# Eight 64x32 array tiles for the per-head products, and a token softmax by 32x32 vector transposes

## The chip, the cores and the metric

The kernel runs on one core of one Trainium2 chip. The metric is the device time of one execution in microseconds (us), as the median of several. Engines are named as the profile names them: PE (TensorE, matrix products), PEld (its weight loads), DVE (VectorE), ACT (ScalarE), POOL (GpSimd). PSUM is the memory to which PE writes the products here; its tiles take one bank or two.

## The reference

Two blocks follow one another. `x` is (8, 8, 512, 64): batch, head, token, feature; `state` is (8, 8, 32, 64).

```python
scores  = x @ state^T / 8        # (B,H,512,32): softmax over the 32 states
xread   = softmax(scores)  @ state
scores2 = state @ x^T / 8        # (B,H,32,512): the same numbers, softmax over the 512 tokens
sread   = softmax(scores2) @ x
out     = concat([xread, sread], token axis)      # 544 rows a batch
h = out.reshape(B*544, 512) @ w_in                # w_in 512 x 2048, w_out 2048 x 512, both float64
return (h * cos(h)) @ w_out
```

For token rows `xread @ w_in` is computed as `softmax(scores) @ (state @ w_in)`: the product of the states with w_in is called `sw`, and the attention weights `aT`.

## The kernel before

A main loop walks the batches in 16 steps of 128 hidden columns. In each step PE makes `h` (two matmuls) and `o` (four); DVE and ACT turn h into g = h cos h. The attention of the next batch is cut into parts that are laid into these steps.

```python
for t in tiles(b):                       # 16 steps f = 0..15
    if line: gate3(line[-1])             # g(t-1) = h * cos        DVE; frees a bank of h (two banks)
    hidden(t)                            # h(t)                    PE
    gate(t)                              # q = round(h/2pi)        DVE twice
    want = (len(work) * (t.f + 1) + NF - 1) // NF
    mid = (n_done + want + 1) // 2
    while n_done < mid:  work[n_done](); n_done += 1      # the mid place
    # ... first batch: two weight tiles are converted from float64; sw of this batch at f = 3, 7, 11
    gate2(t)                             # r, r                    DVE; then Abs, Sin  ACT
    if len(line) > 2: output(line.pop(0))                 # o(t-2) PE
    while n_done < want: work[n_done](); n_done += 1      # the late place, behind r, r
```

The attention parts the change touches (27 of them a batch, with the products):

```python
aps = tile_pool(bufs=2, PSUM)                      # a fresh bank for every part
def scores2(hb):                                   # 4 heads x 32 states on partitions
    for e in range(2):                             # 128x64 array tiles, states block by block with zeros
        matmul(out=s2[64*e:64*e+64, :], lhsT=stT[:, hb, 64*e:64*e+64], rhs=xT[:, 2*hb+e],
               tile_position=(0, 64*e))
    ...                                            # max, subtract
def scores1(ch):                                   # the same scores again, tokens on partitions
    for ci in range(2):
        for k in range(NK):
            matmul(out=s1[:, ...], lhsT=xT[:, k, 2*ch+ci, :], rhs=stT[:, k//2, ...])
    ...                                            # max, subtract
def exps(): activation(z, z, Exp, scale=scale)     # both softmaxes, one 2048-wide instruction
# sums, norm2, turn2 (transposes to a2T), norm1, turn1 (transposes to aT), reads (sT)
def products(nt, hb):                              # sw, 128x64 tiles, one bank each
    ...
```

Of the kernel before, what the change touches and what calls it, by code (L numbers as in the profile page):

```python
# [9 lines left out]
F32 = mybir.dt.float32  # L10
# [16 lines left out]
def kernel(  # L27
# [17 lines left out]
    NHB = H // 4  # L45
# [10 lines left out]
    carry = ctx.enter_context(tc.tile_pool(name="carry", bufs=2))  # L56
    gp = ctx.enter_context(tc.tile_pool(name="gp", bufs=4))
    msb = ctx.enter_context(tc.tile_pool(name="msb", bufs=3))
    osb = ctx.enter_context(tc.tile_pool(name="osb", bufs=2))
    aps = ctx.enter_context(tc.tile_pool(name="aps", bufs=2, space=PSUM))  # L60
# [12 lines left out]

    stB = consts.tile([P, B, NHB, 2 * D], F32)
    nc.vector.memset(stB, 0.0)
    ident = consts.tile([P, P], F32)
    make_identity(nc, ident)
    st_src = state.rearrange("b (hb q) n d -> q n b hb d", q=4)
    for q in range(4):
        j = q % 2  # L80
        nc.sync.dma_start(out=stB[Ns * q:Ns * q + Ns, :, :, D * j:D * j + D],
                          in_=st_src[q])
# [83 lines left out]
    def attention(b):  # L166


        x_b = x_t.pop(b)
        stT = small.tile([P, NHB, P], F32, name="stT")  # L170
        xT = asb.tile([P, NK, NC, P], F32, name="xT")


        N1 = NC * H * Ns
        z = asb.tile([P, N1 + NHB * S], F32, name="z")
        z1 = z[:, 0:N1].rearrange("p (m n) -> p m n", n=Ns)
        z2 = z[:, N1:].rearrange("p (hb t) -> p hb t", hb=NHB)
        mx = small.tile([P, NC * H + NHB], F32, name="mx")
        iz = small.tile([P, NC * H + NHB], F32, name="iz")
        a2T = asb.tile([P, NHB, NC, P], F32, name="a2T")  # L180
        aT = carry.tile([P, NHB, NC, P], F32, name="aT")
        sw = carry.tile([P, NHB, Dff], F32, name="sw")
        aT_of[b], sw_of[b] = aT, sw
        CH = NC // 2

        def states():
            st_ps = aps.tile([P, NHB, P], F32, name="at")
            for hb in range(NHB):
                nc.tensor.transpose(out=st_ps[:, hb, :], in_=stB[:, b, hb, :],
                                    identity=ident)  # L190
            nc.vector.tensor_copy(stT, st_ps)

        def tokens(k):
            xp = aps.tile([P, NC, P], F32, name="at")
            for c in range(NC):
                nc.tensor.transpose(out=xp[:, c, :],  # L196
                                    in_=x_b[:, c, 2 * k:2 * k + 2, :],
                                    identity=ident)
            nc.scalar.copy(xT[:, k], xp)  # L199

        def scores2(hb):
            s2 = aps.tile([P, S], F32, name="at")
            for e in range(2):
                nc.tensor.matmul(  # L204
                    out=s2[64 * e:64 * e + 64, :],
                    lhsT=stT[:, hb, 64 * e:64 * e + 64],
                    rhs=xT[:, 2 * hb + e].rearrange("p c t -> p (c t)"),
                    start=True, stop=True, tile_position=(0, 64 * e))
            m = mx[:, NC * H + hb:NC * H + hb + 1]
            nc.vector.reduce_max(out=m, in_=s2, axis=AX.X)  # L210
            nc.vector.tensor_scalar(z2[:, hb, :], s2, m, None, op0=ALU.subtract)  # L211

        def scores1(ch):
            s1 = aps.tile([P, CH * H, Ns], F32, name="at")
            for ci in range(CH):
                for k in range(NK):
                    e = k % 2
                    nc.tensor.matmul(  # L218
                        out=s1[:, ci * H + 2 * k:ci * H + 2 * k + 2, :],
                        lhsT=xT[:, k, CH * ch + ci, :],  # L220
                        rhs=stT[:, k // 2, 64 * e:64 * e + 64],
                        start=True, stop=True)
            ms = slice(ch * CH * H, (ch + 1) * CH * H)
            nc.vector.reduce_max(out=mx[:, ms], in_=s1, axis=AX.X)
            nc.vector.tensor_tensor(
                z1[:, ms, :], s1,
                mx[:, ms].unsqueeze(2).to_broadcast([P, CH * H, Ns]),
                op=ALU.subtract)

        def exps():  # L230
            nc.scalar.activation(z, z, func=ACTF.Exp, scale=scale)

        def sums():
            nc.vector.reduce_sum(out=iz[:, NC * H:], in_=z2, axis=AX.X)
            nc.vector.reduce_sum(out=iz[:, 0:NC * H], in_=z1, axis=AX.X)
            nc.vector.tensor_scalar(iz, iz, 1e-9, None, op0=ALU.add)
            nc.vector.reciprocal(iz, iz)

        def norm2():
            for hb in range(NHB):  # L240
                nc.vector.tensor_scalar(z2[:, hb, :], z2[:, hb, :],
                                        iz[:, NC * H + hb:NC * H + hb + 1],
                                        None, op0=ALU.mult)

        def norm1():
            nc.vector.tensor_tensor(
                z1, z1,
                iz[:, 0:NC * H].unsqueeze(2).to_broadcast([P, NC * H, Ns]),
                op=ALU.mult)


        def turn2(hb):
            tp = aps.tile([P, NC, P], F32, name="at")
            for c in range(NC):
                nc.tensor.transpose(out=tp[:, c, :],
                                    in_=z2[:, hb, P * c:P * c + P],
                                    identity=ident)
            nc.vector.tensor_copy(a2T[:, hb], tp)  # L258

        def turn1(hb):  # L260
            tp = aps.tile([P, NC, P], F32, name="at")
            for c in range(NC):
                m0 = H * c + 4 * hb
                nc.tensor.transpose(out=tp[:, c, :], in_=z1[:, m0:m0 + 4, :],
                                    identity=ident)
            nc.vector.tensor_copy(aT[:, hb], tp)



        sr = {}  # L270

        def reads(half):
            if half == 0:
                sr[0] = aps.tile([P, NK, 2 * Ns], F32, name="at")
            for k in range(2 * half, 2 * half + 2):
                e = k % 2
                for c in range(NC):
                    nc.tensor.matmul(  # L278
                        out=sr[0][:, k, :], lhsT=x_b[:, c, 2 * k:2 * k + 2, :],
                        rhs=a2T[:, k // 2, c, 64 * e:64 * e + 64],  # L280
                        start=(c == 0), stop=(c == NC - 1))
            if half == 0:
                return
            for j in range(2):
                rows = slice(D * j, D * j + D)
                nc.vector.tensor_copy(sT[rows, :, b, :],
                                      sr[0][rows, :, Ns * j:Ns * j + Ns])


        def products(nt, hb):  # L290
            ps = aps.tile([P, WC], F32, name="at")
            for e in range(2):
                nc.tensor.matmul(  # L293
                    out=ps[64 * e:64 * e + 64, :],
                    lhsT=stT[:, hb, 64 * e:64 * e + 64],
                    rhs=w_in[:, 2 * hb + e, WC * nt:WC * nt + WC],
                    start=True, stop=True, tile_position=(0, 64 * e))
            nc.scalar.copy(sw[:, hb, WC * nt:WC * nt + WC], ps)  # L298

        def part(fn, *args):  # L300
            return lambda: fn(*args)

        attn = [part(states)] + [part(tokens, k) for k in range(NK)]
        attn += [part(scores2, hb) for hb in range(NHB)]
        attn += [part(scores1, ch) for ch in range(2)]
        attn += [exps, sums, norm2]
        attn += [part(turn2, hb) for hb in range(NHB)]
        attn += [norm1]
        attn += [part(turn1, hb) for hb in range(NHB)]
        attn += [part(reads, 0), part(reads, 1)]  # L310
        prod = [part(products, nt, hb) for nt in range(NT)
                for hb in range(NHB)]
        return attn, prod
# [66 lines left out]
    def tiles(b):  # L380
        for f in range(NF):
# [3 lines left out]
            if b < B:  # L385
                t.n, t.kn, t.store = S, NHB, store_x(b)
                t.lhs = lambda i, b=b, cols=cols: sw_of[b][:, i, cols]
                t.rhs = lambda i, b=b: aT_of[b][:, i].rearrange(
                    "p c t -> p (c t)")
# [18 lines left out]

    for i, part in enumerate(attn):
        part()  # L410
        if i % 4 == 3:
            convert_to(n_conv + 1)
    convert_to(NK + 1)
    for part in prod[:NHB]:
        part()
    first = prod[NHB:]

    line = []
    for b in range(B + 1):
# [7 lines left out]
        for t in tiles(b):  # L427
# [10 lines left out]
            if b == 0:  # L438

                convert_to(NK + 1 + 2 * (t.f + 1))  # L440
                if t.f % 4 == 3:
                    for part in first[:NHB]:
                        part()
# [40 lines left out]
```

## Time and profile before

Time before: 1007.9 us (1006.7 to 1008.3). The stretches below are cut at the first h of a batch, as the trace dates it; their sum is the profiled span, 1005.8.

| stretch | us | what sets it |
|---|---|---|
| start, until h of batch 0 | 50.2 | attention of batch 0, first weight tiles |
| first batch | 172.4 | conversion of the weights on DVE, ACT and POOL |
| six batches with the next one's attention | 632.1 | PE, 6 x 105.35 |
| batch 7, no attention | 83.1 | PE |
| state rows | 68.0 | PE and the end |

The profile is read from the coarse to the fine: slices and the chain say who sets the end and when; sums over a stretch say how idle that engine is there; the timeline of one batch gives start-to-start times. In a line of a timeline, the bracket at its end is the time that the engine stood idle just before, and what ended it. The lines stand in the prediction.

### The profile page before, as it was taken

To read this page: it belongs to the slowest core of one execution; us is meant where nothing else is said; L and a number is where in the kernel's file an instruction comes from. 1 tells how busy PE (TensorE), PEld (TensorE's weight loads), DVE (VectorE), ACT (ScalarE), POOL (GpSimd) and SP (SyncE) were. 2 spreads that over 40 slices of the span, in tenths; PEclk is the share of its full clock that TensorE was granted. 3 is DMA by queue.
4 is the path that set the end of the run, shared out by engine and by line. 5 is a ranking of instruction groups with operands and counts; after the bars stand their busy time and mean duration, and the time that the engine had idled before them with its cause. 6 is when DMAs were issued, how large, how long until landed. Compare 5 with 4: busy or idle time off the path is not lost.

```text
span 1005.8 us, 7676 instructions
## 1 busy us (share of the span) xinstructions
PE 932.8 (93%) x2832; PEld 434.8 (43%) x2832; DVE 611.3 (61%) x1011; ACT 360.2 (36%) x554; POOL 88.3 (9%) x70
## 2 busy tenths in 40 slices
PE   4657768699999999999999999999999999999997
PEld 2422324234443455345534454354434443444564
DVE  3567877676754576457644784458446754566553
ACT  2354645553323332343223423233223323222322
POOL 0444444530000000000000000000000000000000
PEclk9576969799999999999999999999999999999999
DMA  8242222401020101010020002010001000100100
GB/s 188 82 128 83 84 84 84 125 1 42 1 42 0 42 0 30 13 42 1 1 42 22 21 1 42 0 42 0 1 1 42 1 1 0 42 0 1 42 1 21
DMA packets 45029, 35.09 MB, mean 35 GB/s; under 512 B 36544, under 2 KB 36544, under 8 KB 44992
## 3 DMA queue, kind: packets, MB, share of 16 engines
q1 hardware_dynamic: 44992, 34.61, 12.3%
q8 instruction: 22, 0.36, 0.1%
q14 instruction: 15, 0.12, 0.0%
HBM read 25.69 MB, written 8.91 MB: 34 GB/s over the span
## 4 chain that ended last, share of the span: by engine, by line
PE 82%; DVE 10%; ACT 3%; POOL 2%; issue 1%; DMA 1%; SPq 0%; POOLq 0%; ACTq 0%
PE o L358 44%; PE h L322 23%; PE at L293 6%; PE at L278 3%; PE at L218 2%; DVE e L155 2%; DVE e L138 2%; DVE r L340 1%; POOL w_in L158 1%; PE at L204 1%; PE at L196 1%; DVE e L153 1%; DVE q L328 1%; DVE fr L144 1%; DVE r L338 1%
## 5 line engine op out<-in xcount | busy, mean ns | idle before, releaser
L358 PE MATMUL o<-w_out,g 128*128 128x512 f32 x1088 | 498.5, 600 | 0.5 <-ACT ot L364 0.5
L358 PEld LDWEIGHTS o<-w_out,g 128*128 128x128 f32 x1088 | 200.8, 191 | 250.4 <-issue 243.5
L322 PE MATMUL h<-aT,sw 128*128 128x512 f32 x512 | 251.5, 614 | 10.7 <-DVE g L348 10.7
L342 ACT ACTIVATE r<-r 128x512 f32<-128x512 f32 (+1 forms) x144 | 87.4, 607 | 383.7 <-DVE r L340 383.7
L348 DVE TENSOR_TENSOR g<-h,r 128x512 f32<-128x512 f32 (+1 forms) x144 | 94.8, 658 | 152.2 <-ACT r L343 151.8
L328 DVE TENSOR_SCALAR q<-h 128x512 f32<-128x512 f32 (+1 forms) x144 | 94.8, 658 | 112.1 <-PE h L322 111.4
L322 PEld LDWEIGHTS h<-aT,sw 128*128 128x128 f32 x512 | 93.2, 194 | 126.0 <-issue 88.7
L340 DVE SCALAR_TENSOR_TENSOR r<-q,r 128x512 f32<-128x512 f32 (+1 forms) x144 | 103.8, 721 | 4.9
L293 PE MATMUL at<-w_in,stT 128*64 128x512 f32 x256 | 82.4, 669 | 22.7 <-DVE a2T L258 6.6
L343 ACT ACTIVATE r<-r,halfpi 128x512 f32<-128x512 f32 (+1 forms) x144 | 100.5, 698 | 4.5
L338 DVE SCALAR_TENSOR_TENSOR r<-q,h 128x512 f32<-128x512 f32 (+1 forms) x144 | 94.3, 655 | 4.4 <-ACT q L331 1.4
L298 ACT COPY sw<-at 128x512 f32<-128x512 f32 x64 | 37.0, 583 | 128.1 <-PE at L293 128.1
L333 DVE TENSOR_SCALAR q<-q 128x512 f32<-128x512 f32 (+1 forms) x128 | 52.5, 410 | 4.4
L293 PEld LDWEIGHTS at<-w_in,stT 128*64 128x64 f32 x256 | 14.8, 143 | 80.0 <-issue 57.2
L152 POOL TENSOR_TENSOR fr<-fr,fl 128x512 f32<-128x512 f32 x32 | 47.4, 1480 | 18.6 <-ACT fl L148 18.6
L141 ACT ACTIVATE e<-e,ebias 128x512 int32<-128x512 int32 x32 | 23.1, 721 | 52.7 <-DVE e L138 52.7
L138 DVE TENSOR_SCALAR e<-raw 128x512 int32<-128x512 int32 x32 | 26.1, 815 | 24.1 <-POOL w_in L158 17.4
L278 PEld LDWEIGHTS at<-a2T,x_b 128*128 128x128 f32 x256 | 34.3, 210 | 7.5 <-issue 7.2
L218 PEld LDWEIGHTS at<-stT,xT 128*128 128x128 f32 x256 | 30.9, 192 | 8.0 <-issue 6.5
L278 PE MATMUL at<-a2T,x_b 128*128 128x64 f32 x256 | 33.6, 290 | 0.0
L196 PE MATMUL at<-ident,x_b 128*128 128x128 f32 x128 | 22.3, 303 | 11.8 <-ACT xT L199 9.5
L218 PE MATMUL at<-stT,xT 128*128 128x64 f32 x256 | 30.3, 272 | 0.2 <-DVE z L211 0.2
(48 smaller groups left out, 471.8 us busy)
## 6 DMA issues: line engine op xcount, KB each, us to landing
x_b<-in_x_dram SPq DMA_DIRECT2D x32, 256.0 KB, 4.6
raw<-in_moe_w_in_dram SPq DMA_DIRECT2D x16, 512.0 KB, 4.0
raw<-in_moe_w_out_dram SPq DMA_DIRECT2D x16, 512.0 KB, 3.3
out_dram<-ot SPq DMA_DIRECT2D x32, 256.0 KB, 2.1
stB<-in_state_dram SPq DMA_DIRECT2D x4, 128.0 KB, 3.2
out_dram<-ot SPq DMA_DIRECT2D x8, 64.0 KB, 1.7
```

Of the source, the lines that this page charges most:

```text
L218: nc.tensor.matmul(out=s1[:, ci * H + 2 * k:ci * H + 2 * k + 2, :], lhsT=xT[:, k, CH * ch + ci, :], rhs=stT[:, k // 2, 64 * e:64 * e + 64] ...
L278: nc.tensor.matmul(out=sr[0][:, k, :], lhsT=x_b[:, c, 2 * k:2 * k + 2, :], rhs=a2T[:, k // 2, c, 64 * e:64 * e + 64], start=(c == 0), stop ...
L293: nc.tensor.matmul(out=ps[64 * e:64 * e + 64, :], lhsT=stT[:, hb, 64 * e:64 * e + 64], rhs=w_in[:, 2 * hb + e, WC * nt:WC * nt + WC], star ...
L322: nc.tensor.matmul(out=t.hp, lhsT=t.lhs(i), rhs=t.rhs(i), start=(i == 0), stop=(i == t.kn - 1))
L328: nc.vector.tensor_scalar(q, t.hp, 1.0 / (2.0 * math.pi), MAGIC, op0=ALU.mult, op1=ALU.add)
L333: nc.vector.tensor_scalar(q, q, MAGIC, None, op0=ALU.subtract)
L338: nc.vector.scalar_tensor_tensor(out=r, in0=t.q, scalar=-C1, in1=t.hp, op0=ALU.mult, op1=ALU.add)
L340: nc.vector.scalar_tensor_tensor(out=r, in0=t.q, scalar=-C2, in1=r, op0=ALU.mult, op1=ALU.add)
L342: nc.scalar.activation(r, r, func=ACTF.Abs)
L343: nc.scalar.activation(r, r, func=ACTF.Sin, bias=halfpi, scale=-1.0)
L348: nc.vector.tensor_tensor(t.g[:, 0:t.n], t.hp, t.r, op=ALU.mult)
L358: nc.tensor.matmul(out=acc[i], lhsT=t.g[:, P * i:P * i + P], rhs=w_out[:, t.f, :], start=(t.f == 0), stop=(t.f == NF - 1))
```

## The change

The intent is to relieve PE. Each head gets its own 64x32 tile of the array (64 features in, 32 states out), so all eight heads multiply side by side, for the scores and for `sw`. The second score product disappears: the softmax over the states is taken from the same scores, states on partitions, by reductions and transposes of 32x32 blocks on DVE. Everything in attention now writes one PSUM tile `at` of two banks.

```diff
-    aps = ctx.enter_context(tc.tile_pool(name="aps", bufs=2, space=PSUM))
+    aps = ctx.enter_context(tc.tile_pool(name="aps", bufs=1, space=PSUM))
...
+    at = aps.tile([P, 2, S], F32, name="at")
...
+        def per_head(rhs):
+            w, r = rhs
+            for k in range(NK):
+                for j in range(2):
+                    nc.tensor.matmul(
+                        out=at[Ns * k:Ns * k + Ns, j, :],
+                        lhsT=w[D * j:D * j + D, b, Ns * k:Ns * k + Ns],
+                        rhs=r(slice(D * j, D * j + D), k),
+                        start=True, stop=True, tile_position=(D * j, Ns * k))
+        def scores():
+            per_head((stS, lambda rows, k: xT[rows, k, :]))
+            nc.vector.tensor_reduce(out=m2, in_=at, op=ALU.max, axis=AX.X, negate=True)
+            nc.vector.tensor_reduce(out=m1..., in_=at..., op=ALU.max, axis=AX.X,
+                                    apply_transpose=True)
+            for j in range(2):
+                nc.scalar.activation(z2[:, j], at[:, j], func=ACTF.Exp,
+                                     bias=m2[:, j:j + 1], accum_out=i2[:, j:j + 1])
+        def shift():
+            spread_of(m1)                       # vector transpose of a broadcast
+            nc.vector.tensor_tensor(z1, at, spread, op=ALU.subtract)
+            nc.scalar.activation(z1, z1, func=ACTF.Exp)
+        # sums: transposing sum of z1, reciprocals; norms: spread, aT = z1 * spread; z2 scaled on ACT
+        attn = [part(tokens, k) for k in range(NK)]
+        attn += [scores, shift, sums, norms]
+        attn += [part(turn, j) for j in range(2)]
+        attn += [part(reads, half) for half in range(2)]
+        prod = [part(products, nt) for nt in range(NT)]
...
     for i, part in enumerate(attn):             # batch 0, ahead of the loop
         part()
-        if i % 4 == 3:
+        if i % 3 == 2:
             convert_to(n_conv + 1)
```

More of the change, by code (lines that the diff above doesn't have):

```diff
@@ L44 @@
     NC = S // P
-    NHB = H // 4
     T = S + Ns
@@ L56 @@
     carry = ctx.enter_context(tc.tile_pool(name="carry", bufs=2))
+    swp = ctx.enter_context(tc.tile_pool(name="swp", bufs=6))
     gp = ctx.enter_context(tc.tile_pool(name="gp", bufs=4))
@@ L70, with states @@
     nc.vector.memset(ebias, -896.0)
-    stB = consts.tile([P, B, NHB, 2 * D], F32)
-    nc.vector.memset(stB, 0.0)
+    st = consts.tile([P, B, 2 * D], F32)
+    stT = consts.tile([P, B, P], F32)
+    stS = consts.tile([P, B, P], F32)
     ident = consts.tile([P, P], F32)
     make_identity(nc, ident)
-    st_src = state.rearrange("b (hb q) n d -> q n b hb d", q=4)
-    for q in range(4):
-        j = q % 2
-        nc.sync.dma_start(out=stB[Ns * q:Ns * q + Ns, :, :, D * j:D * j + D],
-                          in_=st_src[q])
+    st_src = state.rearrange("b (k j) n d -> j k n b d", j=2)
+    for k in range(NK):
+        for j in range(2):
+            queue = nc.sync if j == 0 else nc.scalar
+            queue.dma_start(out=st[Ns * k:Ns * k + Ns, :, D * j:D * j + D],
+                            in_=st_src[j, k])
+    at = aps.tile([P, 2, S], F32, name="at")
+    def states():
+        for half in range(2):
+            for i in range(4):
+                nc.tensor.transpose(out=at[:, half, P * i:P * i + P],
+                                    in_=st[:, 4 * half + i, :], identity=ident)
+            dst = slice(4 * half, 4 * half + 4)
+            src = at[:, half].rearrange("p (b m) -> p b m", b=4)
+            nc.vector.tensor_copy(stT[:, dst], src)
+            nc.scalar.activation(stS[:, dst], src, func=ACTF.Copy, scale=scale)
     x_t = {}
@@ L169, in attention @@
         x_b = x_t.pop(b)
-        stT = small.tile([P, NHB, P], F32, name="stT")
-        xT = asb.tile([P, NK, NC, P], F32, name="xT")
-        N1 = NC * H * Ns
-        z = asb.tile([P, N1 + NHB * S], F32, name="z")
-        z1 = z[:, 0:N1].rearrange("p (m n) -> p m n", n=Ns)
-        z2 = z[:, N1:].rearrange("p (hb t) -> p hb t", hb=NHB)
-        mx = small.tile([P, NC * H + NHB], F32, name="mx")
-        iz = small.tile([P, NC * H + NHB], F32, name="iz")
-        a2T = asb.tile([P, NHB, NC, P], F32, name="a2T")
-        aT = carry.tile([P, NHB, NC, P], F32, name="aT")
-        sw = carry.tile([P, NHB, Dff], F32, name="sw")
-        aT_of[b], sw_of[b] = aT, sw
-        CH = NC // 2
-        def states():
-            st_ps = aps.tile([P, NHB, P], F32, name="at")
-            for hb in range(NHB):
-                nc.tensor.transpose(out=st_ps[:, hb, :], in_=stB[:, b, hb, :],
-                                    identity=ident)
-            nc.vector.tensor_copy(stT, st_ps)
+        xT = asb.tile([P, NK, S], F32, name="xT")
+        z2 = asb.tile([P, 2, S], F32, name="z2")
+        z1 = asb.tile([P, 2, S], F32, name="z1")
+        spread = asb.tile([P, 2, S], F32, name="spread")
+        NB = S // 32
+        m1 = small.tile([P, 2, NB], F32, name="m1")
+        m2 = small.tile([P, 2], F32, name="m2")
+        i2 = small.tile([P, 2], F32, name="i2")
+        a2T = asb.tile([P, 2, NC, P], F32, name="a2T")
+        aT = carry.tile([P, 2, S], F32, name="aT")
+        aT_of[b] = aT
         def tokens(k):
-            xp = aps.tile([P, NC, P], F32, name="at")
+            xp = at[:, k % 2]
             for c in range(NC):
-                nc.tensor.transpose(out=xp[:, c, :],
+                nc.tensor.transpose(out=xp[:, P * c:P * c + P],
                                     in_=x_b[:, c, 2 * k:2 * k + 2, :],
@@ L199, in tokens @@
             nc.scalar.copy(xT[:, k], xp)
-        def scores2(hb):
-            s2 = aps.tile([P, S], F32, name="at")
-            for e in range(2):
-                nc.tensor.matmul(
-                    out=s2[64 * e:64 * e + 64, :],
-                    lhsT=stT[:, hb, 64 * e:64 * e + 64],
-                    rhs=xT[:, 2 * hb + e].rearrange("p c t -> p (c t)"),
-                    start=True, stop=True, tile_position=(0, 64 * e))
-            m = mx[:, NC * H + hb:NC * H + hb + 1]
-            nc.vector.reduce_max(out=m, in_=s2, axis=AX.X)
-            nc.vector.tensor_scalar(z2[:, hb, :], s2, m, None, op0=ALU.subtract)
@@ L213, in scores1 @@
-        def scores1(ch):
-            s1 = aps.tile([P, CH * H, Ns], F32, name="at")
-            for ci in range(CH):
-                for k in range(NK):
-                    e = k % 2
-                    nc.tensor.matmul(
-                        out=s1[:, ci * H + 2 * k:ci * H + 2 * k + 2, :],
-                        lhsT=xT[:, k, CH * ch + ci, :],
-                        rhs=stT[:, k // 2, 64 * e:64 * e + 64],
-                        start=True, stop=True)
-            ms = slice(ch * CH * H, (ch + 1) * CH * H)
-            nc.vector.reduce_max(out=mx[:, ms], in_=s1, axis=AX.X)
-            nc.vector.tensor_tensor(
-                z1[:, ms, :], s1,
-                mx[:, ms].unsqueeze(2).to_broadcast([P, CH * H, Ns]),
-                op=ALU.subtract)
@@ L230, in exps @@
-        def exps():
-            nc.scalar.activation(z, z, func=ACTF.Exp, scale=scale)
-        def sums():
-            nc.vector.reduce_sum(out=iz[:, NC * H:], in_=z2, axis=AX.X)
-            nc.vector.reduce_sum(out=iz[:, 0:NC * H], in_=z1, axis=AX.X)
-            nc.vector.tensor_scalar(iz, iz, 1e-9, None, op0=ALU.add)
-            nc.vector.reciprocal(iz, iz)
-        def norm2():
-            for hb in range(NHB):
-                nc.vector.tensor_scalar(z2[:, hb, :], z2[:, hb, :],
-                                        iz[:, NC * H + hb:NC * H + hb + 1],
-                                        None, op0=ALU.mult)
@@ L245, in norm1 @@
-        def norm1():
-            nc.vector.tensor_tensor(
-                z1, z1,
-                iz[:, 0:NC * H].unsqueeze(2).to_broadcast([P, NC * H, Ns]),
-                op=ALU.mult)
-        def turn2(hb):
-            tp = aps.tile([P, NC, P], F32, name="at")
+        def per_head(rhs):
+            w, r = rhs
+            for k in range(NK):
+                for j in range(2):
+                    nc.tensor.matmul(
+                        out=at[Ns * k:Ns * k + Ns, j, :],
+                        lhsT=w[D * j:D * j + D, b, Ns * k:Ns * k + Ns],
+                        rhs=r(slice(D * j, D * j + D), k),
+                        start=True, stop=True, tile_position=(D * j, Ns * k))
@@ new lines, in scores @@
+        def scores():
+            per_head((stS, lambda rows, k: xT[rows, k, :]))
+            nc.vector.tensor_reduce(out=m2, in_=at, op=ALU.max, axis=AX.X,
+                                    negate=True)
+            nc.vector.tensor_reduce(
+                out=m1.rearrange("p j t -> p (j t)"),
+                in_=at.rearrange("p j (t i) -> p (j t) i", i=32),
+                op=ALU.max, axis=AX.X, apply_transpose=True)
+            for j in range(2):
+                nc.scalar.activation(z2[:, j], at[:, j], func=ACTF.Exp,
+                                     bias=m2[:, j:j + 1],
+                                     accum_out=i2[:, j:j + 1])
@@ new lines, in spread_of @@
+        def spread_of(m):
+            nc.vector.transpose(
+                out=spread.rearrange("p j (t i) -> p (j t) i", i=32),
+                in_=m.rearrange("p j t -> p (j t)").unsqueeze(2)
+                .to_broadcast([P, 2 * NB, 32]))
+        def shift():
+            spread_of(m1)
+            nc.vector.tensor_tensor(z1, at, spread, op=ALU.subtract)
+            nc.scalar.activation(z1, z1, func=ACTF.Exp)
+        def sums():
+            nc.vector.tensor_reduce(
+                out=m1.rearrange("p j t -> p (j t)"),
+                in_=z1.rearrange("p j (t i) -> p (j t) i", i=32),
+                op=ALU.add, axis=AX.X, apply_transpose=True)
+            for v in (m1, i2):
+                nc.vector.tensor_scalar(v, v, 1e-9, None, op0=ALU.add)
+                nc.vector.reciprocal(v, v)
@@ L254, in turn2, with norms, turn @@
+        def norms():
+            spread_of(m1)
+            nc.vector.tensor_tensor(aT, z1, spread, op=ALU.mult)
+            for j in range(2):
+                nc.scalar.activation(z2[:, j], z2[:, j], func=ACTF.Copy,
+                                     scale=i2[:, j:j + 1])
+        def turn(j):
             for c in range(NC):
-                nc.tensor.transpose(out=tp[:, c, :],
-                                    in_=z2[:, hb, P * c:P * c + P],
+                nc.tensor.transpose(out=at[:, j, P * c:P * c + P],
+                                    in_=z2[:, j, P * c:P * c + P],
@@ L257, in turn2 @@
                                     identity=ident)
-            nc.vector.tensor_copy(a2T[:, hb], tp)
-        def turn1(hb):
-            tp = aps.tile([P, NC, P], F32, name="at")
-            for c in range(NC):
-                m0 = H * c + 4 * hb
-                nc.tensor.transpose(out=tp[:, c, :], in_=z1[:, m0:m0 + 4, :],
-                                    identity=ident)
-            nc.vector.tensor_copy(aT[:, hb], tp)
-        sr = {}
+            nc.vector.tensor_copy(a2T[:, j].rearrange("p c m -> p (c m)"),
+                                  at[:, j])
@@ L272, in reads @@
         def reads(half):
-            if half == 0:
-                sr[0] = aps.tile([P, NK, 2 * Ns], F32, name="at")
-            for k in range(2 * half, 2 * half + 2):
-                e = k % 2
+            sr = at[:, half, 0:4 * Ns].rearrange("p (k m) -> p k m", k=2)
+            for i in range(2):
+                k = 2 * half + i
                 for c in range(NC):
                     nc.tensor.matmul(
-                        out=sr[0][:, k, :], lhsT=x_b[:, c, 2 * k:2 * k + 2, :],
-                        rhs=a2T[:, k // 2, c, 64 * e:64 * e + 64],
+                        out=sr[:, i, :], lhsT=x_b[:, c, 2 * k:2 * k + 2, :],
+                        rhs=a2T[:, :, c, Ns * k:Ns * k + Ns],
@@ L281, in reads @@
                         start=(c == 0), stop=(c == NC - 1))
-            if half == 0:
-                return
+            ks = slice(2 * half, 2 * half + 2)
             for j in range(2):
                 rows = slice(D * j, D * j + D)
-                nc.vector.tensor_copy(sT[rows, :, b, :],
-                                      sr[0][rows, :, Ns * j:Ns * j + Ns])
-        def products(nt, hb):
-            ps = aps.tile([P, WC], F32, name="at")
-            for e in range(2):
-                nc.tensor.matmul(
-                    out=ps[64 * e:64 * e + 64, :],
-                    lhsT=stT[:, hb, 64 * e:64 * e + 64],
-                    rhs=w_in[:, 2 * hb + e, WC * nt:WC * nt + WC],
-                    start=True, stop=True, tile_position=(0, 64 * e))
-            nc.scalar.copy(sw[:, hb, WC * nt:WC * nt + WC], ps)
+                nc.vector.tensor_copy(sT[rows, ks, b, :],
+                                      sr[rows, :, Ns * j:Ns * j + Ns])
@@ L300, in part, with products @@
+        def products(nt):
+            cols = slice(WC * nt, WC * nt + WC)
+            per_head((stT, lambda rows, k: w_in[rows, k, cols]))
+            sw_of[b, nt] = swp.tile([P, 2, WC], F32, name="sw")
+            nc.scalar.copy(sw_of[b, nt], at)
         def part(fn, *args):
             return lambda: fn(*args)
-        attn = [part(states)] + [part(tokens, k) for k in range(NK)]
-        attn += [part(scores2, hb) for hb in range(NHB)]
-        attn += [part(scores1, ch) for ch in range(2)]
@@ L306, in attention @@
-        attn += [exps, sums, norm2]
-        attn += [part(turn2, hb) for hb in range(NHB)]
-        attn += [norm1]
-        attn += [part(turn1, hb) for hb in range(NHB)]
-        attn += [part(reads, 0), part(reads, 1)]
-        prod = [part(products, nt, hb) for nt in range(NT)
-                for hb in range(NHB)]
+        attn = [part(tokens, k) for k in range(NK)]
+        attn += [scores, shift, sums, norms]
+        attn += [part(turn, j) for j in range(2)]
+        attn += [part(reads, half) for half in range(2)]
@@ L385, in tiles @@
             if b < B:
-                t.n, t.kn, t.store = S, NHB, store_x(b)
-                t.lhs = lambda i, b=b, cols=cols: sw_of[b][:, i, cols]
-                t.rhs = lambda i, b=b: aT_of[b][:, i].rearrange(
-                    "p c t -> p (c t)")
+                t.n, t.kn, t.store = S, 2, store_x(b)
+                part = slice(P * f % WC, P * f % WC + P)
+                t.lhs = lambda i, b=b, nt=P * f // WC, part=part: (
+                    sw_of[b, nt][:, i, part])
+                t.rhs = lambda i, b=b: aT_of[b][:, i]
             else:
@@ L407, in convert_to @@
             n_conv += 1
+    states()
     for i, part in enumerate(attn):
         part()
-        if i % 4 == 3:
+        if i % 3 == 2:
             convert_to(n_conv + 1)
     convert_to(NK + 1)
-    for part in prod[:NHB]:
-        part()
-    first = prod[NHB:]
+    prod[0]()
+    first = prod[1:]
     line = []
@@ L440 @@
                 convert_to(NK + 1 + 2 * (t.f + 1))
-                if t.f % 4 == 3:
-                    for part in first[:NHB]:
-                        part()
-                    first = first[NHB:]
+                if t.f % 4 == 3 and first:
+                    first.pop(0)()
             gate2(t)
```

## The prediction

> **What bounds the kernel now.** I read the page's slices and chain first, then the sums over stretches, then the timelines of PE, DVE and ACT inside one batch.
>
> ```profile
> PE   4657768699999999999999999999999999999997
> ...
> PEclk9576969799999999999999999999999999999999
> ...
> PE 82%; DVE 10%; ACT 3%; POOL 2%; issue 1%; DMA 1%; SPq 0%; POOLq 0%; ACTq 0%
> ```
>
> From slice 9 on PE is at 9 in every slice at full clock, and the chain is 82% PE; only the first 8 or 9 slices (conversion of the f64 weights) are something else.
>
> ```profile
> 219.00:870.00 651.00, 650.53 (x2024) 296.44 (x2023) 391.81 (x631) 217.69 (x321) 0.00 (x0) 1.00 0.06 17
> ```
>
> Columns: stretch, us, then busy us of PE, PEld, DVE, ACT, POOL, then clock, DMA share, GB/s. PE has 0.5 us of idle in 651; DVE is 60% busy, ACT 33%. The chain in order of time repeats itself: `o x8` starts at 330.08, 435.43 and 540.78, so one batch with the next batch's attention beside it takes 105.35 us. There are six such batches (223 to 855). Before them lie the start (0 to 50) and the first batch (50 to 223, weights still converting), after them batch 7 without attention (855 to 938) and the state rows (938 to 1006).
>
> What PE does in the period, from its timeline (start, us, engine, line, operation, count):
>
> ```profile
> 426.87 1.98 PE L322 MATMUL h<-aT,sw 128*128 128x512 f32 x4
> 428.78 1.08 PE L293 MATMUL at<-w_in,stT 128*64 128x512 f32 x4
> 429.79 3.70 PE L358 MATMUL o<-w_out,g 128*128 128x512 f32 x8
> 433.33 1.88 PE L322 MATMUL h<-aT,sw 128*128 128x512 f32 x4
> ...
> 472.19 1.88 PE L322 MATMUL h<-aT,sw 128*128 128x512 f32 x4
> 473.91 3.60 PE L358 MATMUL o<-w_out,g 128*128 128x512 f32 x8
> 477.35 1.88 PE L322 MATMUL h<-aT,sw 128*128 128x512 f32 x4
> ```
>
> Starts, not durations, are to be subtracted, since neighbours overlap. An f32 matmul is two passes, so x4 is two matmuls. A bare f step is h 1.72 (472.19 to 473.91) and o 3.44: 5.16 us. Beside an array-tile group h takes 1.91 and o 3.54 to 3.63. The group itself takes 1.01 (428.78 to 429.79): four 512-column passes of 0.43 each would need 1.72 one after another, so its two 128x64 tiles do run at the same time (2 x 0.43), and the remainder is switching. With the 0.1 lost on each side a group costs 1.21.
>
> The second limit is the gate loop: DVE and ACT pass one tile back and forth.
>
> ```profile
> 484.88 0.69 DVE L348 TENSOR_TENSOR g<-h,r 128x512 f32<-128x512 f32 x1 [0.61 <-ACT r L343]
> 485.49 0.68 DVE L328 TENSOR_SCALAR q<-h 128x512 f32<-128x512 f32 x1
> 486.20 0.43 DVE L333 TENSOR_SCALAR q<-q 128x512 f32<-128x512 f32 x1
> 486.54 1.22 DVE L246 TENSOR_TENSOR z<-z,iz 128x1024 f32<-128x1024 f32 x1
> 487.68 0.68 DVE L338 SCALAR_TENSOR_TENSOR r<-q,h 128x512 f32<-128x512 f32 x1
> ...
> 490.54 0.69 DVE L348 TENSOR_TENSOR g<-h,r 128x512 f32<-128x512 f32 x1 [0.68 <-ACT r L343]
> 491.14 0.68 DVE L328 TENSOR_SCALAR q<-h 128x512 f32<-128x512 f32 x1
> ```
>
> From q to q is 5.65 us, of which the 1024-wide multiply placed between q and r takes 1.14: the bare loop is 4.51 us, only 0.65 below PE's 5.16. Whatever sits between q and r comes on top; what sits after r hides behind ACT's Abs and Sin. A table switch is on this loop as well:
>
> ```profile
> 471.75 0.63 ACT L342 ACTIVATE r<-r 128x512 f32<-128x512 f32 x1 [1.20 <-DVE r L340]
> 472.39 1.28 ACT L343 ACT_TABLE_LOAD   x1
> 473.69 0.72 ACT L343 ACTIVATE r<-r,halfpi 128x512 f32<-128x512 f32 x1
> ```
>
> **What the Trainium skill says.** "TensorEngine Tiling (Array Packing)", Tiling Modes: 64x32 gives eight tiles, different tiles load and multiply in parallel, and changing the mode drains the engine. The trace agrees for two 128x64 tiles (above), with 0.35 us beyond two passes as the price. "TensorE: Matmul & The Clock Gate", Part 3: sixteen 32x32 tiles measured 10.6 times, each further tile about 4 ns; no run here shows eight f32 tiles yet. "Vector Engine (DVE) Microarchitecture Reference", 3.8: the 32x32 transpose sustains one element per cycle and lane. No transpose is in this trace; at that rate a 1024-wide one should cost what the 1024-wide reductions do here (1.21). "ScalarE: Activation LUTs", What ACT_TABLE_LOAD costs: 1283 ns and a drain of 1380. The trace has the 1283, but Sin starts 1.30 after the load starts: no such drain, and I use 1.30.
>
> **The change part by part, for one of the six batches.**
> - PE before: 16 x 5.16 = 82.5; ten tile groups (8 products, 2 scores2) x 1.21 = 12.1; scores1 2 x 1.73 = 3.5; transposes of x, states and z 1.74 + 0.22 + 1.74 = 3.7; reads 2 x 1.73 = 3.5. Sum 105.2, measured 105.35.
> - PE after: steps 82.5; five groups of eight tiles (4 products, 1 scores), each two passes and a switch plus six more tiles at 7 ns (the stagger of the pair here), an estimate of 1.26: 6.3; scores1 gone; transposes of x 1.74 and of z2 only, 0.87; reads 3.5. Sum 94.8, a saving of 10.5.
> - DVE: attention was 14.6 us a batch (rows L191 to L286 over 8). After: two maxima, a subtraction, a sum, two spreads and a multiply, all 1024 wide at about 1.2, two copies at 0.69 and small ones: about 11. It is less in sum, but where it sits matters. The work list is now 16 parts for 16 steps, and the code's rounding puts every part in the mid place, between q and r. Before, 27 parts were split over both places.
> - ACT: exponentials now come in two parts in two steps (scores, then shift), so Sin's table is reloaded in two steps instead of one.
>
> Gate loop of the burst, q to q: scores 4.5 + 2.4 (two maxima) + 1.3 (Sin's load) + 0.2 = 8.4; shift 4.5 + 1.15 + 1.2 + 1.3 = 8.15; sums 4.5 + 1.2 + 0.85 = 6.55; norms 4.5 + 2.35 = 6.85; turn 5.15. PE offers 6.45, then 5.16 three times, then 5.6. Taking h of the scores step as 0, its q starts at 1.9. The q's follow at 10.3, 18.5, 25.05 and 31.9. With two h banks, h two steps on waits for the g just ahead of that q. PE alone would start h at 6.45, 11.6, 16.75. The step after next (10.3 against 11.6) still fits, then 18.5 against 16.75: 1.75 lost; 25.05 against 23.65: 1.4; 31.9 against 30.7: 1.2; after that PE leads again. About 4.4 us of PE idle a batch, on about 95: 99.3, so 6 us saved, times six **36 us**.
>
> Start: 1.8 us of memset and the second score product go and state loads are split over two queues, but x's transfer, the exponential and the cold reads (7 us) stay; the fourth w_in tile still ends it. I estimate 4 us. First batch: its loop is DVE, ACT and POOL converting, about 10.5 us for two weight tiles, plus attention on that loop. Less DVE work is set against one more table reload and all parts in mid: 0, give or take 6. Batch 7 and the state rows have no attention: 0. Sum: 1007.9 - 36 - 4 = **968 us**.
>
> **Rivals.** (1) PE stays the only bound, because ACT or DVE work is shorter or the slack larger than I count: 6 x 10.5 + 4 = 67 saved, 941. For it: no stall in the present burst, though DVE runs q to q without a pause from 474 to 491. Against: 5.16 against 8 in two consecutive steps. (2) The transposing reductions and spreads run slower than 1.2 (no row for them here). Each 1 us more on all four adds up to 4 us a batch: 992. (3) The two row halves do not run together: five groups at two more passes, 0.86 x 5 = 4.3 a batch, partly on top of the stalls: 985 to 994. (4) The eight tiles run one after another: 5 x 6.9 = 34 instead of 6.3, far slower. The overlapping pair speaks against it.
>
> **Range and chances.** The centre takes the loop as counted; 945 is nearly all of rival 1, 992 one of rivals 2 and 3. Faster by over 2% means below 987.7: 0.82. Same, two of the bad terms together: 0.13. Slower needs rival 4 or something unseen: 0.05.
>
> **What will show it.** A group of eight tiles (x16) should take 1.0 to 1.1 start to start; 1.9 would be rival 3. PE's idle in 223 to 840 should be some 25 us, its releaser DVE g, all in the three or four steps after scores, not in products; none would be rival 1. The batch period should read about 99; spreads and transposing reductions 1.1 to 1.3 each; two Sin table loads a batch; h of the first batch at 45 to 47. Wrong rows for these are what would make the prediction wrong.

## The result

The changed kernel takes 992.1 us (989.6 to 993.3, 4 runs) against 1007.8 before. Ratios here are with a 95% interval; they are not always quite the ratio of the medians. Here it is 0.9842, interval 0.9822 to 0.9863. That is a gain of 1.6%, clear of the noise, and 24 us above the predicted 968.

By stretches, from the starts of h:

| stretch | before | predicted | changed | above prediction |
|---|---|---|---|---|
| start | 50.2 | 46 | 54.9 | 9 |
| first batch | 172.4 | 172 | 180.3 | 8 |
| six batches | 632.1 | 596 | 604.1 | 8 |
| batch 7 and state rows | 151.1 | 151 | 150.8 | 0 |

The page of the changed kernel, busy tenths of PE and granted clock in 40 slices, and the chain by engine:

```profile
PE   3545828598989997999899989998999899999997
...
PEclk9987978799999999999999989999999899999999
...
PE 64%; DVE 22%; ACT 9%; POOL 2%; issue 2%; DMA 1%; ACTq 0%; POOLq 0%; DVEq 0%
```

PE is no longer at 9 in every slice: an 8 (once a 7) comes back once a batch, and the chain has given 18 points of PE to DVE and ACT. The sums over the stretch of the six batches, same columns as before:

```profile
235.00:839.00 604.00, 582.88 (x1969) 259.60 (x1968) 364.48 (x583) 233.75 (x332) 0.00 (x0) 0.98 0.07 18
```

21 us of PE idle where there was half a microsecond, and a clock of 0.98. The timeline of PE in one batch:

```profile
359.94 1.09 PE L211 MATMUL at<-xT,stS 64*32 64x512 f32 x16
360.95 3.70 PE L345 MATMUL o<-w_out,g 128*128 128x512 f32 x8
...
371.49 3.60 PE L345 MATMUL o<-w_out,g 128*128 128x512 f32 x8
377.88 1.98 PE L309 MATMUL h<-aT,sw 128*128 128x512 f32 x4 [2.79 <-DVE g L335]
379.70 3.60 PE L345 MATMUL o<-w_out,g 128*128 128x512 f32 x8
384.37 1.98 PE L309 MATMUL h<-aT,sw 128*128 128x512 f32 x4 [1.07 <-DVE g L335]
```

The intended part works: eight tiles, sixteen passes, in 1.01 us from start to start. With what h and o lose beside it a products step lasts 6.37, so the group costs 1.21, as much as two tiles cost before. Then h waits for g in the steps behind shift, as foretold, but for longer. DVE and ACT show where the time is, the steps of scores and shift:

```profile
361.13 1.22 DVE L221 TENSOR_REDUCE m<-at 128x2 f32<-128x1024 f32 x1
362.27 1.24 DVE L223 TRANSPOSE_TENSOR_REDUCE m<-at 128x32 f32<-128x1024 f32 x1
363.44 0.65 DVE L325 SCALAR_TENSOR_TENSOR r<-q,h 128x512 f32<-128x512 f32 x1
364.12 0.69 DVE L327 SCALAR_TENSOR_TENSOR r<-q,r 128x512 f32<-128x512 f32 x1
368.92 0.69 DVE L335 TENSOR_TENSOR g<-h,r 128x512 f32<-128x512 f32 x1 [4.11 <-ACT r L330]
```

```profile
363.59 1.28 ACT L228 ACT_TABLE_LOAD   x1 [5.12 <-DVE m L223]
364.89 0.69 ACT L228 ACTIVATE z<-at,m 128x512 f32<-128x512 f32 x1
...
366.23 0.63 ACT L329 ACTIVATE r<-r 128x512 f32<-128x512 f32 x1
366.87 1.28 ACT L330 ACT_TABLE_LOAD   x1
```

ACT's table load for the exponential waits for L223, the second reduction, although the exponential needs only the first, L221. The load and the two exponentials then hold ACT from 363.59 to 366.23, so Abs starts 1.4 us after its r is ready (364.81), and DVE stands idle for 4.11 us in front of g. From q to q the four loops are 9.49, 8.21, 6.49 and 6.94 us; the prediction had 8.4, 8.15, 6.55 and 6.85.

One thing more on PE, from another batch:

```profile
579.04 3.78 PE L309 MATMUL h<-aT,sw 128*128 128x512 f32 x4 [2.80 <-DVE g L335]
582.61 4.90 PE L345 MATMUL o<-w_out,g 128*128 128x512 f32 x8
```

After the wait of 2.8 us, h takes 3.78 instead of 1.98: the clock record has half clock here, for 3.4 or 6.8 us in five of the six batches. "TensorE: Matmul & The Clock Gate" of the Trainium skill, Part 1, says that the gate falls back to half clock after an idle window of about 3.4 us and opens again after a busy one. The trace agrees on the half clock and on steps of 3.4 us, though the wait listed is only 2.8, and in one batch (377.88, above) it brought no half clock. It accounts for most of the difference between the 34 us that the six batches spend above PE's own need (604.1 against 569.9, below) and the 21 us of idle listed: the one batch at full clock lists 4.95 us of waits (2.79, 1.07, 1.09), the five others 2.8 to 3.5, as PE, working slowly, asks for g later. Six times 4.95 would be 30. The time hardly depends on it: the two batches with 6.8 us of half clock take 100.9, the others, with 3.4 or none, 100.6.

Last the start, PE and POOL:

```profile
11.02 1.12 PE L200 MATMUL at<-ident,x_b 128*128 128x128 f32 x4 [1.49 <-ACT stS L97]
12.81 1.12 PE L200 MATMUL at<-ident,x_b 128*128 128x128 f32 x4 [0.68 <-ACT xT L203]
...
51.89 1.92 PE L211 MATMUL at<-w_in,stT 64*32 64x512 f32 x4 [2.39 <-POOL w_in L173]
54.92 3.78 PE L309 MATMUL h<-aT,sw 128*128 128x512 f32 x4 [1.11 <-ACT sw L290]
```

The transposes of the second head pair wait until ACT has copied the first pair out of `at`, though they go into its other half. And the first h waits for the fourth w_in tile, which POOL finishes only at 51.83, where the kernel before had it at 49.07.

### The profile page after: what moved, and what is told of

Its sections match the earlier page's. It is cut to its first block, busy times and chain, and to the rows that moved or that the text cites. A ratio compares the mean times of both kernels' runs of the same rounds, so it can differ in the third digit from the quotient of the medians.

```text
span 990.2 us, 7635 instructions
## 1 busy us (share of the span) xinstructions
PE 868.8 (88%) x2824; PEld 395.7 (40%) x2824; DVE 593.6 (60%) x972; ACT 390.9 (39%) x586; POOL 86.7 (9%) x70
## 4 chain that ended last, share of the span: by engine, by line
PE 64%; DVE 22%; ACT 9%; POOL 2%; issue 2%; DMA 1%; ACTq 0%; POOLq 0%; DVEq 0%
PE o L345 35%; PE h L309 20%; PE at L211 4%; PE at L275 3%; DVE r L327 3%; ACT r L330 2%; DVE e L170 2%; DVE q L315 2%; DVE e L153 2%; ACT r L329 2%; ACT L330 2%; POOL w_in L173 2%; DVE g L335 2%; DVE r L325 2%; DVE spread L233 2%
## 5 line engine op out<-in xcount | busy, mean ns | idle before, releaser
L345 PE MATMUL o<-w_out,g 128*128 128x512 f32 x1088 | 504.8, 606 | 0.4 <-ACT ot L351 0.4
L309 PE MATMUL h<-aT,sw 128*128 128x512 f32 x512 | 259.0, 630 | 53.9 <-DVE g L335 52.8
L345 PEld LDWEIGHTS o<-w_out,g 128*128 128x128 f32 x1088 | 204.1, 194 | 254.4 <-issue 246.6
L309 PEld LDWEIGHTS h<-aT,sw 128*128 128x128 f32 x512 | 99.0, 198 | 188.5 <-issue 106.9
L315 DVE TENSOR_SCALAR q<-h 128x512 f32<-128x512 f32 (+1 forms) x144 | 94.8, 658 | 93.7 <-PE h L309 93.7
L211 PE MATMUL at<-w_in,stT 64*32 64x512 f32 x512 | 47.6, 646 | 35.8 <-POOL w_in L173 18.1
L290 ACT COPY sw<-at 128x1024 f32<-128x1024 f32 x32 | 32.3, 1009 | 82.6 <-PE at L211 82.6
L203 ACT COPY xT<-at 128x512 f32<-128x512 f32 x32 | 18.7, 585 | 42.4 <-PE at L200 42.4
L211 PEld LDWEIGHTS at<-w_in,stT 64*32 64x32 f32 x512 | 6.9, 108 | 68.3 <-POOL w_in L173 26.9
L309 PE MATMUL h<-sT,w_in 128*128 128x256 f32 x128 | 30.2, 379 | 0.0
L309 PEld LDWEIGHTS h<-sT,w_in 128*128 128x128 f32 x128 | 24.3, 190 | 10.1 <-issue 7.4
```

Source lines behind the costliest of these rows:

```text
L211: nc.tensor.matmul(out=at[Ns * k:Ns * k + Ns, j, :], lhsT=w[D * j:D * j + D, b, Ns * k:Ns * k + Ns], rhs=r(slice(D * j, D * j + D), k), st ...
L309: nc.tensor.matmul(out=t.hp, lhsT=t.lhs(i), rhs=t.rhs(i), start=(i == 0), stop=(i == t.kn - 1))
L315: nc.vector.tensor_scalar(q, t.hp, 1.0 / (2.0 * math.pi), MAGIC, op0=ALU.mult, op1=ALU.add)
L345: nc.tensor.matmul(out=acc[i], lhsT=t.g[:, P * i:P * i + P], rhs=w_out[:, t.f, :], start=(t.f == 0), stop=(t.f == NF - 1))
```

## The experiments

The theory after the first look: the six batches lose to a burst of parts on the gate loop, of which one term was too small (the exponential waits for the second reduction); the first batch loses to the same burst, in a loop that also converts weights; the start loses to the single tile `at` and to a conversion that comes too late. All kernels below gave correct results.

### late_all: every part behind the second half of the gate

```diff
-            mid = (n_done + want + 1) // 2
+            mid = n_done
```

> The only edit: the attention parts run after the second half of the gate (behind r, r) instead of between its halves; same instructions. Theory (the burst of reductions sits on the gate loop, so h waits for g): DVE work then lies beside ACT's Abs and Sin, the waits of h for DVE g go from about 5.8 us a batch to under 1, the period from 100.6 to about 95.5, and the six batches save about 30 us; the first batch may gain too, as its loop holds the same burst: 950 to 965 us. Rival (there is simply too much DVE and ACT work beside the gate, or the loss is on PE): period stays near 100, about 990 us.

Measured: 947.8 us, ratio 0.9408 (0.9394 to 0.9422), a little better than the 950 to 965 expected. The periods are 94.99 in all six batches, against 94.8 for PE alone in the prediction; no wait of h for g is left in them, and the sum over the six batches reads

```profile
227.00:796.00 569.00, 568.83 (x1968) 256.50 (x1966) 368.23 (x582) 232.10 (x332) 0.00 (x0) 1.00 0.07 19
```

Columns as before: PE busy 568.83 of 569 with the same 582 or so instructions on DVE, clock 1.00. In the scores step DVE now does

```profile
347.30 0.69 DVE L325 SCALAR_TENSOR_TENSOR r<-q,h 128x512 f32<-128x512 f32 x1
348.02 0.69 DVE L327 SCALAR_TENSOR_TENSOR r<-q,r 128x512 f32<-128x512 f32 x1
350.71 1.23 DVE L221 TENSOR_REDUCE m<-at 128x2 f32<-128x1024 f32 x1 [1.99 <-PE at L211]
351.85 1.24 DVE L223 TRANSPOSE_TENSOR_REDUCE m<-at 128x32 f32<-128x1024 f32 x1
353.01 0.65 DVE L335 TENSOR_TENSOR g<-h,r 128x512 f32<-128x512 f32 x1
```

The reductions stand between r and g, beside Abs and Sin, not in front of them. Start 55.1, first batch 171.4 (from 180.3), six batches 569.9 (from 604.1). The rival, too much work in sum, is ruled out: the work is the same.

### late_rest: the same, but not in the first batch

```diff
-            mid = (n_done + want + 1) // 2
+            mid = n_done if b else (n_done + want + 1) // 2
```

> As late_all, but the first batch keeps the parts between the halves of the gate. Theory: period about 95.5 in the six batches, the first batch stays at 180 us: about 962 us, and late_all minus this run is what the place costs the first batch. Rival (place does not matter): about 990 us.

Measured: 958.2 us, ratio 0.9511 (0.9497 to 0.9525). Six batches 569.9, first batch 180.8. So the mid place costs the first batch 9.4 us and nothing else does: with late parts it takes 171.4, within 1 us of the kernel before (172.4). The waits listed there for PE's h on g are 31.7 us in the changed kernel, 7.5 in late_all and 10.7 in the kernel before.

### inter: the same parts in the mid place, in another order

```diff
-            work = attn + prod
+            work = attn[:6] + prod[:1] + attn[6:7] + prod[1:2] + attn[7:8] + prod[2:3]
+            work += attn[8:] + prod[3:]
```

> Same instructions in the same place of a step, but the list of parts is mixed: a products part before sums, before norms and before the first turn, so that PE has 1.2 us more in the steps between the slow ones. Theory (a burst that outruns the slack of two h banks): the wait in the step after shift stays (about 2.9 us), the two later waits (about 1.3 and 1.4) vanish, period about 97.7, about 974 us. Rival (the sum of the work counts, not its order): unchanged, 990 us.

Measured: 964.8 us, ratio 0.9571 (0.9555 to 0.9587), period 96.7, better than the 97.7 expected. The two later waits are gone, and the first has become another one. This is the only wait of PE listed in the six batches (us in total, times, longest):

```profile
PE at L211 <- DVE z L240: 9.5, 6, 1.6
```

The products part has moved into the step where PE used to wait and takes 1.2 us of that time for itself; it then waits for the subtraction that still reads `at`. The order counts, not the sum.

### m1late: the transposing maximum moves from scores to shift

```diff
         def scores():
-            nc.vector.tensor_reduce(out=m1..., in_=at..., op=ALU.max, axis=AX.X, apply_transpose=True)
         def shift():
+            nc.vector.tensor_reduce(out=m1..., in_=at..., op=ALU.max, axis=AX.X, apply_transpose=True)
             spread_of(m1)
```

> The maximum over states (the transposing reduction) moves from the scores step to the head of the shift step; same instructions. Theory: in the changed kernel ACT's exponentials wait for this second reduction, because readers of the one tile at on two engines follow one another in program order; without it in front the scores loop falls from 9.5 to about 7.2 us and shift rises from 8.2 to 9.3, in sum 1.2 less, period about 99.3, about 984 us. Rival (the 1.1 us that scores took above my count are the accumulator reads or something else on ACT): sum of the two steps unchanged, 991 us.

Measured: 987.9 us, ratio 0.9802 (0.9787 to 0.9817; unclear against the kernel before at the 2% line, but all four runs lie below all four of the changed kernel). In the six batches as expected: from q to q the scores loop is 6.98 (expected 7.2) and the shift loop 9.50 (9.3), in sum 16.5 against 17.7, the period 99.35 against 100.6, which is 8.0 us in six batches. ACT in the scores step:

```profile
361.18 1.28 ACT L224 ACT_TABLE_LOAD   x1
365.08 0.69 ACT L224 ACTIVATE z<-at,m 128x512 f32<-128x512 f32 x1 [2.62 <-DVE m L221]
```

The exponential now waits for L221, and its table load has no wait in front. The total misses 984, since the start (56.3) and the first batch (182.9) got longer by 3.9 us together. The trace shows where the 1.3 us of the start come from. In batch 0, ahead of the loop, nothing stands between scores and shift, and DVE does

```profile
23.42 1.25 DVE L235 TRANSPOSE_TENSOR_REDUCE m<-at 128x32 f32<-128x1024 f32 x1 [1.51 <-ACT z L224]
```

The second reduction needs nothing of the exponentials but now waits for them, the reverse of the wait in the changed kernel (23.18, ACT on L223). So two readers of the tile `at` on different engines are put in program order by the framework, whichever comes first. Of the 2.6 us in the first batch, some 1.5 arise in the shift step, where the moved reduction now stands (m1late lags by 1.75 us at L221 and by 3.25 at L240); no run tests that.

A possible reason for such an order: "PSUM — Partial Sum Buffer" of the Trainium skill, "PSUM bank collisions raise a hardware error", says that any two engines on one bank and 32-partition quadrant collide, two readers included, and that a dependency is needed. No run here shows a collision, as none was allowed; that DVE and ACT never read `at` at once agrees with the page.

### before_late: the edit of late_all on the kernel before

> The kernel before with the edit of late_all (parts behind the second half of the gate). Theory (before, PE alone bounds the six batches, with no wait of h for g): period stays 105.35, so 632 us for the six, whatever the place; only the first batch (172.4 us), whose loop holds these parts, may change, by some us either way: 1000 to 1012 us. Rival (late is a gain of its own that any version of this kernel would have): some 30 us faster.

Measured: 1050.9 us, ratio 1.0434 (1.0419 to 1.0448), which neither theory expected. The period goes from 105.35 to 110 or 111.7 (the three batches of 111.7 have 3.4 us of half clock, the three of 110 have none), the first batch from 172.4 to 182.7. DVE and PE in one batch:

```profile
497.71 1.22 DVE L234 TENSOR_REDUCE iz<-z 128x2 f32<-128x1024 f32 x1 [4.66 <-ACT z L231]
```

```profile
501.27 1.98 PE L322 MATMUL h<-aT,sw 128*128 128x512 f32 x4 [2.43 <-DVE g L348]
```

There exps and sums are two parts that fall in one step, so DVE stands 4.66 us in front of a sum that needs the 2048-wide exponential, with g queued behind it, and h waits for g. In other steps norm1 and turn1 meet (PE waits 2.87 us for z). So late is not a gain of its own. Between these two kernels the difference is that late_all has one part a step, so that what a part needs from another engine was made a step earlier; no run varies that alone.

### conv: batch 0 converts after every second part

```diff
-        if i % 3 == 2:
+        if i % 2 == 1:
             convert_to(n_conv + 1)
```

> Only the start is touched: a weight conversion is issued after every second attention part of batch 0 instead of every third (six calls in its twelve parts, not four). Theory (h of the first batch starts at 54.9 instead of 50.2 because four calls leave the fourth w_in tile to be converted after the reads, where nothing hides it): w_in's fourth tile is ready before the reads end at about 44, h starts at about 48 to 49, about 986 us. Rival (the start is set by the attention chain of batch 0 itself): h stays at 54 to 55, or later by the DVE work put into the chain.

Measured: 982.8 us, ratio 0.9758 (0.9744 to 0.9771). The fourth w_in tile is ready at 40.5 and the reads end at 45.3; h starts at 49.0 instead of 54.9. The first batch gains 2.9 too, as it begins with one more tile converted. The six batches stay at 603.7.

### banks: batch 0 uses free banks in place of the single tile

```diff
-            xp = at[:, k % 2]
+            xp = ops.tile([P, S], F32, name="o") if b == 0 else at[:, k % 2]
```

and the same for the PSUM target of turn and reads.

> Only the start is touched: batch 0's token transposes, turns and reads write fresh PSUM tiles of the output pool (idle then) instead of the one tile at; conversions as in the changed kernel. Theory (the single tile at lets PE and the copy behind it run only in turn, 1.8 us a token part): the token parts take about 2 us less, turns and reads about 1.5 less, the scores product starts at about 16.5 instead of 18.55, the reads end 3 to 4 us earlier, h starts at about 51, about 988 us. Rival (conversion alone sets the start): attention ends earlier but h stays within 1 us of 54.9.

Measured: 987.1 us, ratio 0.9801 (0.9787 to 0.9814). The sixteen transposes run as one block from 9.2 to 13.3, scores start at 13.2 (expected 16.5), and the reads end at 38.7 instead of 43.8. h starts at 49.85, 5.1 us earlier. The products then wait for w_in, 1.95 and 2.39 us, so conversion still ends the start. The edit frees the token transposes, turns and reads at once; their shares were not separated.

### both: the two together

> conv and banks together. If the two are separate links of one chain they add: h at about 45, about 982 us. If one hides behind the other, h is where the better one of the two alone put it.

Measured: 975.6 us, ratio 0.9688 (0.9675 to 0.9701). h starts at 42.9 (expected 45): 12.0 us earlier than in the changed kernel, against 5.9 and 5.1 for the two alone. They add, with one more microsecond, as separate links of one chain would.

### best: late_all with both

> late_all with the two edits of the start (conv and banks) together. If start, first batch and six batches are separate stretches, their gains add: h of the first batch at 43, first batch about 169 us, six batches 570 us, the rest as before (83 and 68 us): about 934 us. If the late place undoes what an earlier start gives the first batch (its conversions then still set its end), about 945 us.

Measured: 932.9 us, ratio 0.9243 (0.9226 to 0.926). Start 43.8, first batch 167.1, six batches 569.9, the rest 150.9: the gains add. This beats the kernel before by 7.6% and the changed one by 6%.

## Why the prediction was wrong

The direction was right, the mechanism in the six batches was right, the size was not: 16 us gained instead of 40. Three terms failed, with 8 or 9 us each: the scores step of the gate loop, the first batch, and the start.

- **PE's part, right.** 94.8 us of PE work a batch were predicted (its terms add up to 94.9); late_all, where nothing but PE is left, has 94.99. The group was put at 1.26 and costs 1.21. Rivals 3 and 4 are excluded, and rival 1 by the waits.
- **The waits of h for g, right in place, short in size.** The batch at full clock lists 2.79, 1.07 and 1.09 us where 1.75, 1.4 and 1.2 were predicted; its period is 5.6 above PE alone (100.6 less 94.99), not 4.4. The step that failed is the term "scores 4.5 + 2.4 + 1.3 + 0.2 = 8.4": it leaves 0.2 for everything that the exponentials put into the loop, which fits only if they start after the first reduction. They start after the second, since both engines read `at`; Abs comes 1.4 us late, and the loop is 9.49. m1late took that wait away, and the period fell to 99.35, where the prediction had 99.3. That is 8 of the 24 us. The match of 99.35 is a little lucky: m1late's waits are 3.86, not 4.4, and another 0.5 a batch lies outside them.
- **Transposes on DVE, right.** 1.24 each, against 1.2. Rival 2 is out. Two Sin table loads a batch and no drain, also as said.
- **First batch, wrong.** "0, give or take 6" was 7.8. The step that failed is "less DVE work is set against one more table reload and all parts in mid": the loop was not added up. late_rest and late_all show that the place alone is worth 9.4 there: the parts in the mid place are on the path in this loop too.
- **Start, wrong in sign.** Predicted 4 us shorter, it is 4.7 longer. Two terms are missing. Nothing in the prediction stands for waits on `at`: PE waits for the copy of the other half (banks: 5.1). And "the fourth w_in tile still ends it" was right, but when that tile is ready was not worked out. Both kernels call the conversion four times between the parts of batch 0. Before, the last of them came with three parts still to follow; in the changed kernel it comes after the last part, so that the third and the fourth tile are both finished after the reads (conv: 5.9).
- **Two slips of reading.** DVE does not run "without a pause from 474 to 491": it stands idle for 1.45, 0.61 and 0.68 us in front of three g, the last two in lines that the prediction shows. And PE's terms before add up to 105.3, not 105.2. Nothing rests on either.
- **Not foreseen:** half clock after waits of 2.8 us. It costs at most 0.4 us a batch here (100.9 against 100.6).

What stays open: why m1late lengthens the first batch by 2.6 us, and how banks' 5.1 us divide among the parts.

## What to carry to other kernels

When an engine is relieved, count the loop that comes next step by step, and look at where a part stands in it: behind the last instruction that another engine waits for, the attention parts cost the six batches nothing beyond PE's own work here; ahead of it the same parts took 34 us. Check that place again for each version, since the same move made the older kernel 4% slower. A tile that parts share acted as one buffer here, also for its readers: draw the waits between engines from the program, not from what the data need.

## What the Trainium skill lacked or had wrong

- "ScalarE: Activation LUTs", What ACT_TABLE_LOAD costs: a drain of 1380 ns beside the 1283 ns of the load. No run here has it: Sin starts 1.30 us after its load does, in the kernel before (472.39 to 473.69) and after.
- "TensorE: Matmul & The Clock Gate", Part 1: half clock after an idle window of about 3.4 us. Here waits listed with 2.8 us were followed by half clock in five of six batches.
- The same page, Part 3, measures packings up to sixteen 32x32 tiles. Not there: eight 64x32 tiles in f32 need two passes of 0.43 us and 1.01 from start to start, and 1.21 with what the neighbours lose to the switch, the same as two 128x64 tiles.
- "PSUM — Partial Sum Buffer" gives the hazard of two readers but not the price of the order that avoids it: 1.2 us a batch here (100.6 against 99.35 in m1late), in a loop.
- No page has the duration of a reduction with a built-in transpose: 1.24 us for 128x1024 f32, as much as a plain one (1.22) or a block transpose (1.24).
